# Casting k's main rows into DRAM in blocks of 16 KB instead of 4 KB

## The chip, the cores and the metric

The kernel runs on one core of a Trainium2 chip. The core has a matrix engine (TensorE, PE in the profile, with its weight loads as PEld), VectorE (DVE), ScalarE (ACT), GpSimd (POOL) and SyncE (SP), and 16 DMA engines that carry out the transfers which SP, ACT and POOL issue. Each engine works through its own list of instructions in order and waits for others by semaphores. The metric is the device time in microseconds (us).

## The reference

Eight batches of random-feature attention over 576 positions and 8 heads of 64, followed by a token-and-channel mixer:

```python
def phi(x):                                   # x: b h 576 64, scaled by 64 ** -0.25
    h = einsum('bhsd,md->bhsm', x, omega) - sum(x * x, -1, keepdims=True) / 2
    return exp(h - max(h, -1, keepdims=True)) / sqrt(128)
q_p, k_p = phi(q_s), phi(k_s)
kv, z = einsum('bhsm,bhsd->bhmd', k_p, v), sum(k_p, axis=2)
x = einsum('bhsm,bhmd->bhsd', q_p, kv) / (einsum('bhsm,bhm->bhs', q_p, z)[..., None] + 1e-6)
x = x.transpose(0, 2, 1, 3).reshape(8, 576, 512)
h = maximum(x.transpose(0, 2, 1) @ w_tok1, 0) @ w_tok2      # mixes positions, 576 -> 256 -> 576
u = x + h.transpose(0, 2, 1)
out = u + maximum(u @ w_ch1, 0) @ w_ch2                     # mixes channels, 512 -> 1536 -> 512
```

## The kernel before

The matrix work is in fp16 with sums in fp32. A batch b goes through attention, the token mixer and the channel mixer. The stages of neighbouring batches are interleaved: TensorE computes the channel mixer of one batch between the attention steps of the next. The interleaving is written out by hand: every step is a job, and the list `ORDER` gives the order in which all jobs are recorded, so each engine's list of instructions is fixed. TensorE has no choice at run time. If the next matmul's operand is late, it waits, and all its later work waits with it.

Attention needs q and k with the 64 head dimensions on the partitions. Batches 0 and 1 are transposed on TensorE from natural loads. For batches 2 to 7 the function `load_transposed` goes through DRAM. A DMA issued by POOL casts fp32 to fp16 into a scratch tensor `scratch[w, b]` of 2304 rows of 128 fp16 values (two positions of 64 side by side). Then SP issues a transposing DMA (line 400, `back`), which writes `kT` or `qT` with 128 partitions. The casts are these:

- q: one DMA of the whole batch (line 379, `cast`), 32 pieces of 9216 values.
- k's main rows (line 384, `cast_main`), the first 512 positions of each of the 8 heads: 512 KB of fp16 from 1 MB of fp32.
- k's tail rows (line 390, `cast_tail`): the last 64 positions, two DMAs of 32 KB, each from four heads.

`back` for k waits for the main cast and both tail casts; `back` for q waits for the q cast. SP's list is in order too. It holds, beside the kT and qT transposes, the transposes `uT<-u` (line 824), which turn the token mixer's output into the stationary operand of the channel mixer, and part of the output stores. POOL's list holds all casting DMAs (v, the casts above, the v tails `vt`), and between them the products `vs` and other elementwise work that waits for DVE.

On TensorE, line 571 (k's tail rows) and line 679 (k's main rows) read `kT`; lines 641 and 691 read `qT`; line 1144 reads `uT` for the channel mixer of batches 1 to 4 and line 1073 for later ones. `kT`, `qT` and `uT` have three buffers each.

Of the kernel before, what the change touches and what calls it, by code (L numbers as in the profile page):

```python
# [137 lines left out]
class Planner:  # L138
# [38 lines left out]
    def place(self, tag, name):  # L177
        return self.held[tag, name]
# [7 lines left out]
def kernel(  # L186
# [14 lines left out]
    B, H, S, D = q.shape  # L201
# [4 lines left out]
    P = 128  # L206
    SM = 512
    ST = S - SM
    NJ = SM // P
# [4 lines left out]
    R = SM // 2  # L214
# [84 lines left out]
    scratch = {}  # L299
# [3 lines left out]
    src = {"q": q, "k": k}  # L303
# [26 lines left out]
    def dma(eng, key, wire, fn, deps=(), take=(), give=(), cost=None):  # L330
        cost = (0.75 if eng == "POOL" else 0.45) if cost is None else cost
        job = add(eng, cost, key, fn, deps, take, give, wire=wire)
        return job
# [41 lines left out]
    def load_transposed(b, key, deps=()):  # L375
        casts = {"q": [], "k": []}
        for n, w in enumerate("qk"):
            def cast(w=w):
                nc.gpsimd.dma_start(
                    out=scratch[w, b].rearrange("(p r) e -> p (r e)", p=P),  # L380
                    in_=src[w][b].rearrange("h s d -> (h s d)").rearrange("(p f) -> p f", p=P),
                )
            def cast_main(w=w):
                nc.gpsimd.dma_start(
                    out=scratch[w, b][0 : H * R].rearrange("(h c r) e -> c h (r e)", h=H, c=P // H),
                    in_=src[w][b, :, 0:SM, :].rearrange("h s d -> h (s d)").rearrange("h (c f) -> c h f", c=P // H),
                )
            def cast_tail(w=w):
                for g in range(2):
                    nc.gpsimd.dma_start(  # L390
                        out=scratch[w, b][H * R : H * RA, g * D : (g + 1) * D],
                        in_=src[w][b, 4 * g : 4 * g + 4, SM:S, :],
                    )
            if w == "k":
                casts[w].append(dma("POOL", key + 0.01 * n - 0.005, 0.8, cast_tail, deps, cost=1.1))
            casts[w].append(dma("POOL", key + 0.01 * n, 3.2, cast if w == "q" else cast_main, deps, cost=0.55))
        for n, w in enumerate("qk"):
            def back(w=w):
                t = (t_qT if w == "q" else t_kT)[place(w + "T", b)]
                nc.sync.dma_start_transpose(out=t.unsqueeze(1), in_=scratch[w, b])  # L400
            ld[w + "T", b] = dma("SP", key + 0.2 + 0.01 * n, 2.2, back, deps=casts[w], take=[(w + "T", b)], cost=2.5)
# [25 lines left out]
    def clear(t):  # L427
# [6 lines left out]
        out=w1m.rearrange("p j t -> p (j t)"), in_=moe_w_tok1[0:SM, :].rearrange("(p j) t -> p (j t)", j=NJ)))  # L434
# [23 lines left out]
    for i in range(2):  # L458
        c0 = i * (NCB // 2)
        j_wc2.append(dma("POOL", -3.0 + 0.1 * i, 3.85, lambda c0=c0: nc.gpsimd.dma_start(  # L460
            out=wc2[:, c0 : c0 + NCB // 2, :], in_=moe_w_ch2[c0 * P : (c0 + NCB // 2) * P, :].rearrange("(i p) d -> p i d", p=P))))
# [5 lines left out]
    for out_, a, b in ((T1, W12, W11), (T2, W22, T1), (T3, W22, W12), (T4, W21, T2)):  # L467
# [3 lines left out]
        out=omega16.rearrange("p (i d) -> p i d", i=2), in0=omega_nat.unsqueeze(1).broadcast_to((P, 2, D)), scalar1=c_scale, scalar2=None, op0=ALU.mult), deps=j_om)  # L471
# [779 lines left out]
```

## Time and profile before

| | before |
|---|---|
| median of 3 runs | 274.45 us (273.89 to 274.65) |
| the profiled execution's own time | 273.79 us |
| its span, first to last instruction | 272.0 us |
| granted TensorE clock, mean | 0.998 |
| TensorE busy | 262.9 us, 97% of the span |
| VectorE, ScalarE, POOL busy | 84%, 60%, 49% of the span |
| DMA moved | 39.70 MB in 81296 packets |
| the six casts of k's main rows | 512 KB each, median 7.1 us from issue to landing |

The profile shows one execution. Times in it are us from the span's start. A row of the timeline gives start, duration, engine, line of the kernel, operation, and what is written from what. Sequencer rows (SPq, and POOL's DMA rows) show the issuing instruction alone; the time to landing is given apart. The DMA share of a window is the busy share of all 16 DMA engines together, where 1.00 is 16 engines busy with one packet each; packets of two queues can overlap on one engine, which gives shares above 1.

### The profile page before, as it was taken

What the parts mean: (1) busy time and instruction counts of PE and PEld (TensorE: products, weight loads), DVE (VectorE), ACT (ScalarE), POOL (GpSimd) and SP (SyncE); (2) the same over time, 40 slices, a digit from 0 to 9 for tenths busy, and PEclk for the clock granted to TensorE, in tenths of its full rate; (3) what the DMA queues carried; (4) which work ended last, traced back from release to release, by engine and by line L of the source; (5) the groups of instructions that cost most, each with busy time, mean ns of one, the idle gap of its engine ahead of it and who ended that gap; (6) DMA issues with size and microseconds to landing.
All of it is one profiled execution on the core that took longest, in us unless ns stands there. A gap on an engine that the chain in (4) does not pass through costs nothing.

```text
span 272.0 us, 6648 instructions
## 1 busy us (share of the span) xinstructions
PE 262.9 (97%) x2647; PEld 180.0 (66%) x2647; DVE 227.2 (84%) x479; ACT 164.2 (60%) x361; POOL 134.6 (49%) x146
## 2 busy tenths in 40 slices
PE   7799999999999999999999999999999999999992
PEld 4367455444568655766578546986789688888881
DVE  3897879876998799987889799899997795799992
ACT  2999941188695338736746865699947541573500
POOL 8895492064803490079459996964145044600001
PEclk9999999999999999999999999999999999999999
DMA  8999999999999999989989986980260063030134
GB/s 199 190 208 210 191 210 185 216 202 132 180 204 156 223 187 175 164 160 158 171 178 173 194 233 64 182 167 2 49 128 2 23 193 58 0 157 0 63 133 119
DMA packets 81296, 39.70 MB, mean 146 GB/s; under 512 B 63984, under 2 KB 77040, under 8 KB 81072
## 3 DMA queue, kind: packets, MB, share of 16 engines
q0 software_dynamic: 31744, 17.74, 44.2%
q1 hardware_dynamic: 46928, 15.37, 29.5%
q10 hardware_dynamic: 2592, 6.16, 6.4%
q8 instruction: 20, 0.33, 0.5%
q14 instruction: 12, 0.10, 0.1%
HBM read 35.95 MB, written 16.52 MB: 193 GB/s over the span
## 4 chain that ended last, share of the span: by engine, by line
PE 86%; DMA 8%; POOL 3%; DVE 1%; issue 0%; POOLq 0%; SPq 0%
PE bank L961 24%; PE bank L1144 19%; PE bank L1073 13%; PE bank L803 5%; PE bank L816 5%; DMA uT<-u 4%; DMA w1m<-in_moe_w_tok_dram 4%; PE bank L1178 4%; PE bank L679 3%; PE bank L768 3%; PE bank L735 3%; PE bank L691 2%; POOL r L339 1%; PE bank L870 1%; PE bank L842 1%; PE bank L854 1%
## 5 line engine op out<-in xcount | busy, mean ns | idle before, releaser
L1144 PE MATMUL bank<-uT,wc 128*128 128x512 f16 x232 | 56.0, 379 | 0.0
L315 POOL TENSOR_TENSOR vs<-v,vs 128x512 f16<-128x512 f16 x31 | 33.1, 1072 | 42.8 <-DVE vs L716 33.5
L310 ACT ACTIVATE r<-bank 128x512 f16<-128x512 f32 (+1 forms) x61 | 34.5, 598 | 26.5 <-PE bank L1144 16.0
L961 PEld LDWEIGHTS <-r 128*128 128x128 f16 x384 | 36.7, 98 | 7.2 <-issue 1.6
L534 ACT ACTIVATE kp<-bank 128x512 f16<-128x512 f32 x64 | 35.5, 623 | 9.6 <-PE bank L679 8.9
L712 DVE TENSOR_REDUCE km<-kp 128x8 f16<-128x1024 f16 x32 | 38.5, 1204 | 2.0 <-ACT kp L534 2.0
L534 ACT ACTIVATE qp<-bank 128x512 f16<-128x512 f32 x64 | 36.5, 620 | 4.3 <-PE bank L691 4.3
L1144 PEld LDWEIGHTS <-wc 128*128 128x128 f16 x232 | 20.5, 98 | 20.1 <-issue 1.1
L961 PEld LDWEIGHTS <-S 128*128 128x128 f16 x288 | 27.7, 98 | 4.7 <-issue 0.4
L786 DVE TENSOR_TENSOR x<-bank,rc 128x320 f16<-128x320 f32 x53 | 25.2, 483 | 1.1
L941 DVE TENSOR_TENSOR o<-u,bank 128x512 f32<-128x512 f16 x28 | 19.1, 680 | 5.8 <-PE bank L961 5.3
L961 PE MATMUL bank<-T,r 128*128 128x256 f16 x192 | 23.8, 273 | 0.0
L961 PE MATMUL bank<-T,S 128*128 128x256 f16 x192 | 23.4, 272 | 0.0
L961 PE MATMUL bank<-wc,r 128*128 128x256 f16 x192 | 23.1, 273 | 0.0
L312 DVE TENSOR_SCALAR r<-bank 128x512 f16<-128x512 f32 (+1 forms) x29 | 18.9, 661 | 3.1 <-PE bank L1144 2.4
L819 DVE TENSOR_TENSOR u<-x,bank 128x512 f16<-128x512 f16 x28 | 17.9, 681 | 1.9 <-PE bank L816 1.9
L315 POOL TENSOR_TENSOR vbd<-vt,vbd 128x512 f16<-128x512 f16 x6 | 6.4, 1060 | 23.5 <-DVE vbd L616 18.5
L768 PEld LDWEIGHTS <-qp 128*128 128x128 f16 x256 | 14.0, 98 | 5.9 <-issue 0.3
L1073 PE MATMUL bank<-uT,wc 128*128 128x256 f16 x120 | 16.6, 273 | 0.6 <-DMA uT<-u 0.6
L941 DVE TENSOR_TENSOR o<-o,bank 128x512 f32<-128x512 f32 x21 | 14.3, 680 | 3.1 <-PE bank L961 2.9
L775 DVE RECIPROCAL rc<-bank 128x5 f32<-128x5 f32 x64 | 11.2, 184 | 6.7 <-PE bank L770 3.7
L768 PE MATMUL bank<-kvsb,qp 128*128 128x65 f16 x256 | 16.0, 193 | 0.2 <-ACT qp L534 0.2
(151 smaller groups left out, 551.3 us busy)
## 6 DMA issues: line engine op xcount, KB each, us to landing
out_dram<-o ACTq DMA_DIRECT2D x9, 512.0 KB, 3.7
q<-in_q_dram POOLq DMA_DIRECT2D x6, 576.0 KB, 7.6
wc<-in_moe_w_ch_dram POOLq DMA_DIRECT2D x4, 768.0 KB, 11.1
k<-in_k_dram POOLq DMA_DIRECT2D x6, 512.0 KB, 7.1
v<-in_v_dram POOLq DMA_DIRECT2D x6, 512.0 KB, 8.6
out_dram<-o SPq DMA_DIRECT2D x5, 512.0 KB, 3.1
r<-in_q_dram POOLq DMA_DIRECT2D x4, 288.0 KB, 7.1
v<-in_v_dram POOLq DMA_DIRECT2D x4, 256.0 KB, 8.9
```

The costliest lines, as they stand in the source:

```text
L310: nc.scalar.activation(out=out, in_=in_, func=AF.Relu)
L312: nc.vector.tensor_relu(out=out, in_=in_)
L315: (nc.gpsimd if eng == "POOL" else nc.vector).tensor_tensor(**kw)
L534: nc.scalar.activation(out=out, in_=in_, func=AF.Exp, bias=0.0, scale=1.0)
L712: nc.vector.reduce_max(out=t_km[place("km", (b, hp))], in_=src_, axis=AX.X)
L768: nc.tensor.matmul(ps[:, k, j * 65 : (j + 1) * 65], st, s[:, i, 0 : D + 1], start=True, stop=True)
L786: nc.vector.tensor_tensor(out=to, in0=ps, in1=rc.unsqueeze(2).broadcast_to((P, NJ + 1, D)), op=ALU.mult)
L819: nc.vector.tensor_tensor(out=t_u[place("u", b)][:, j, :], in0=t_x[place("x", b)][:, j, :], in1=bank(n), op=ALU.add)
L941: nc.vector.tensor_tensor(out=o, in0=a, in1=ps, op=ALU.add)
L961: nc.tensor.matmul(ps[:, j * DH : (j + 1) * DH], a[:, cb, j * P : (j + 1) * P], w[:, cb, :], start=(bank_of(b, j0) not in held and j == j0 ...
L1073: nc.tensor.matmul(ps[:, n, :], w(a)[:, (2 * m + n) * P : (2 * m + n + 1) * P], x_[:, a], start=(what in ("P1", "P2", "P5") and n == 0 and ...
L1144: nc.tensor.matmul(ps, wc1[:, db, cb * P : (cb + 1) * P], moving(db), start=(db == 0), stop=(db == ND - 1))
```

## The change

`cast_main` walks the same bytes in another shape. A head's 512 positions are 32768 consecutive values in the source, and 256 consecutive rows of 128 in the scratch tensor. Before, they were cut into `c = P // H = 16` blocks of 2048 values (4 KB of fp16, 8 KB of fp32); now into `c = NJ = 4` blocks of 8192 values (16 KB of fp16, 32 KB of fp32). The block index c is the outermost dimension of both access patterns, the head the next, and the block's values the innermost.

```diff
             def cast_main(w=w):
                 nc.gpsimd.dma_start(
-                    out=scratch[w, b][0 : H * R].rearrange("(h c r) e -> c h (r e)", h=H, c=P // H),
-                    in_=src[w][b, :, 0:SM, :].rearrange("h s d -> h (s d)").rearrange("h (c f) -> c h f", c=P // H),
+                    out=scratch[w, b][0 : H * R].rearrange("(h c r) e -> c h (r e)", h=H, c=NJ),
+                    in_=src[w][b, :, 0:SM, :].rearrange("h s d -> h (s d)").rearrange("h (c f) -> c h f", c=NJ),
                 )
```

No instruction is added, removed or moved on any engine; only the pattern of the six DMAs of line 384 is another. At the first of them POOL's list reads as follows, with the line, the operation, the names of what is written and read (the name's last numbers are buffers; `k_2_152` is the scratch tensor of batch 2) and the counts of the written pattern, outermost first:

```order
 L315 TENSOR_TENSOR T<-vt_94,T 128x16x64
 L315 TENSOR_TENSOR vs_105<-v_91,vs_105 128x8x64
-L384 DMA k_2_152<-in_k_dram 16x8x2048
+L384 DMA k_2_152<-in_k_dram 4x8x8192
 L315 TENSOR_TENSOR vs_103<-v_91,vs_103 128x8x64
 L371 DMA vt_93<-in_v_dram 64x4x64
```

Nothing moved here; the outermost count went from 16 to 4, the innermost from 2048 to 8192. The other five casts of k's main rows differ in the same way.

## The prediction

> **What bounds the kernel now.** I read the engines' busy times first, then what TensorE waits for, then the DMA issues, and last the places where a cast of k ends in something that TensorE reads.
>
> ```profile
> PE 262.9 (97%) x2647; PEld 180.0 (66%) x2647; DVE 227.2 (84%) x479; ACT 164.2 (60%) x361; POOL 134.6 (49%) x146
> ```
>
> This row of the page is the busy time of each engine, its share of the span and its instructions. TensorE is busy for 97% of the span. The list of TensorE's waits has seven rows, of which these are the longest and the longest one on a DMA:
>
> ```profile
> PE bank L1218 <- DVE S L1215: 1.2, 1, 1.2
> ...
> PE bank L1073 <- DMA uT<-u: 0.6, 2, 0.3
> ```
>
> The columns are the total in us, the number of waits and the longest. TensorE never waits more than 1.2 us, and never for a DMA into kT or qT. So any delay of an operand beyond its slack is added to the time one for one: there is no idle time on TensorE in which it could be made up. The question is how much later the casts land and how much slack stands behind each.
>
> **What one cast costs.** A window in which a cast of k's main rows has the DMA engines to itself, then the q cast and the k cast of the issue table:
>
> ```profile
> 90.20:92.20 2.00, 2.00 (x22) 1.34 (x21) 1.65 (x3) 0.96 (x4) 0.75 (x2) 1.00 0.99 200
> ```
> ```profile
> q<-in_q_dram POOLq DMA_DIRECT2D x6, 576.0 KB, 7.6
> ...
> k<-in_k_dram POOLq DMA_DIRECT2D x6, 512.0 KB, 7.1
> ```
>
> The window's last two numbers are the DMA share, 0.99 of 16 engines, and 200 GB/s written. 524,288 bytes at 200 GB/s are 2.6 us, with all 16 engines at work. Size of block alone changes little: the q cast, in blocks of 18 KB, moves 12% more bytes and lands in 7% more time (7.6 against 7.1 us). What matters is how many of the 16 engines share the work when the outermost count is 4 and not 16. The trace names no engine of a packet, so I bound it from both sides. Low end: the 32 blocks are dealt to 16 engines, two each; 2.6 us, no change. High end: one engine for each outermost index, four engines at a sixteenth of 200 GB/s each, 50 GB/s, so 10.5 us, that is 7.9 us more. The nearest row to an outermost count of 4 is the tail cast, whose source pattern begins with four heads, against the v tail, whose pattern begins with 64 or more:
>
> ```profile
> L390 POOL DMA_DIRECT2D k<-in_k_dram x12: 816/850/897, 40.0 to 162.2; - x12
> ...
> DMA to landing us min/median/max: 5.1/6.8/8.9
> ```
> ```profile
> L371 POOL DMA_DIRECT2D vt<-in_v_dram x16: 615/676/754, 3.9 to 180.9; - x16
> ...
> DMA to landing us min/median/max: 2.3/5.9/11.1
> ```
>
> Both move 32 KB in pieces of 128 bytes. The v tail can land in 2.3 us, the tail cast never in less than 5.1. One writes to SBUF and one to DRAM, so it is no proof, but it points to fewer engines. I take the high end, 7.9 us.
>
> The Trainium skill, "DMA: Bandwidth & Descriptors", section on why a DMA increments its semaphore by 16, says that a transfer runs on the largest number of engines, up to 16, that divides the outermost count of both patterns. By that rule the new cast has four engines and the sum is the one below. No row of this profile shows the number itself.
>
> **Where the casts end.** POOL's issues of the six casts, and what SP does with them:
>
> ```profile
> 36.12 0.60 POOL L384 DMA_DIRECT2D k<-in_k_dram  x1
> ...
> 60.30 0.56 POOL L384 DMA_DIRECT2D k<-in_k_dram  x1
> ...
> 87.22 0.59 POOL L384 DMA_DIRECT2D k<-in_k_dram  x1
> ...
> 99.59 0.58 POOL L384 DMA_DIRECT2D k<-in_k_dram  x1
> ...
> 122.37 0.56 POOL L384 DMA_DIRECT2D k<-in_k_dram  x1
> ...
> 147.41 0.57 POOL L384 DMA_DIRECT2D k<-in_k_dram  x1
> ```
> ```profile
> 47.81 2.71 SPq L400 DMA_TRANSPOSE kT<-k  x1
> 50.57 2.34 SPq L400 DMA_TRANSPOSE qT<-q  x1
> 54.30 1.73 SPq L824 DMA_TRANSPOSE uT<-u  x1
> ...
> 66.27 3.30 SPq L400 DMA_TRANSPOSE qT<-q  x1
> 69.75 3.20 SPq L400 DMA_TRANSPOSE kT<-k  x1
> ...
> 93.93 3.15 SPq L400 DMA_TRANSPOSE kT<-k  x1
> 110.41 3.12 SPq L824 DMA_TRANSPOSE uT<-u  x1
> 113.71 2.88 SPq L400 DMA_TRANSPOSE kT<-k  x1
> ...
> 135.63 5.13 SPq L400 DMA_TRANSPOSE kT<-k  x1
> ...
> 170.63 3.18 SPq L400 DMA_TRANSPOSE kT<-k  x1
> ```
>
> Landing times (shortest, median, longest) of all casts of line 384, of all kT and qT transposes of line 400, and of all uT transposes of line 824, in this order:
>
> ```profile
> L384 POOL DMA_DIRECT2D k<-in_k_dram x6: 557/574/601, 36.1 to 147.4; - x6
> ...
> DMA to landing us min/median/max: 6.5/7.1/9.2
> ```
> ```profile
> DMA to landing us min/median/max: 4.5/6.7/9.3
> ```
> ```profile
> DMA to landing us min/median/max: 5.1/5.6/6.4
> ```
>
> And the first use on TensorE in batches 2, 3 and 4 (kT, uT; qT, kT; kT):
>
> ```profile
> 54.84 0.29 PE L571 MATMUL bank<-omT,kT 64*128 64x128 f16 x4
> ...
> 60.50 1.69 PE L1144 MATMUL bank<-uT,wc 128*128 128x512 f16 x7
> ```
> ```profile
> 74.03 0.28 PE L641 MATMUL bank<-qT,omT 64*128 64x256 f16 x2
> ...
> 78.05 0.61 PE L679 MATMUL bank<-omT,kT 64*128 64x128 f16 x16
> ```
> ```profile
> 107.38 0.39 PE L679 MATMUL bank<-omT,kT 64*128 64x128 f16 x8
> ```
>
> The casts' own times of issue hardly move (POOL spends about 0.57 us on each either way). Each lands 7.9 us later. What else POOL issues behind a cast (q cast, v, tails) stands behind it on the four engines.
>
> **Batch 2.** Issue at 36.12 and the median of 7.1 give a landing at 43.2; with 7.9 more, 51.1. SP starts kT at 47.81 in the profile, so 3.3 us later. kT landing at 51.1 plus 4.5 (the shortest transpose) to 6.7 is at 55.6 to 57.8, against 54.84: a stall of 0.8 to 3.0 us. SP's list goes on behind it: qT starts at 51.1 + 2.71 = 53.8 at the earliest, uT at 53.8 + 2.34 = 56.2, and uT lands 5.6 us later, at 61.8, against 60.50; 1.3 us, of which the first stall is a part. The q cast and the v load are queued behind k's cast on the four engines and hold them when these transposes come, so I take the upper end, 3.0.
>
> **Batch 3.** The longest landing, 9.2 us, belongs to this cast: 60.30 + 9.2 = 69.5, just ahead of kT at 69.75. Now 77.4. kT then lands at 81.9 to 84.1 for a first use at 78.05: 3.9 to 6.1 us. Before that, qT (issued at 66.27) runs into the cast: four of the 16 engines are busy till 77, and a transpose is complete when its last engine is. If its part on the four engines waits for the cast, it lands no earlier than about 77 + 2 (less than the shortest transpose's 4.5, since the other engines' part is done), for a use at 74.03: 5 us, in which kT's delay is contained at its middle value. I take 5.0 for both.
>
> **Batch 4.** kT starts at 93.93, 6.7 us after the cast's issue at 87.22 and so, with a median landing of 7.1, as soon as the cast has landed; now 101.8. kT lands 4.5 to 9.3 us later, at 106.3 to 111.1, against 107.38: 0 to 3.7 us. I take 2.0.
>
> **Batches 5 to 7.** Batch 5's cast, issued at 99.59, lands at 106.7 (median) to 108.8 (longest), now 114.6 to 116.7; kT starts at 113.71 at present, up to 3 us earlier. The first uses in batches 5 and 6:
>
> ```profile
> 128.49 0.62 PE L679 MATMUL bank<-omT,kT 64*128 64x128 f16 x16
> ```
> ```profile
> 144.59 0.28 PE L571 MATMUL bank<-omT,kT 64*128 64x128 f16 x4
> ```
>
> 128.49 hides batch 5. But uT, issued at 110.41 and landing at 115.5 to 116.8, runs into the longer cast, as qT does in batch 3: 0 to 2 us, taken as 1.0. Batch 6: 122.37 + 7.1 + 7.9 = 137.4 against a start at 135.63, 1.8 us late, for a use at 144.59; with 6.7 us to land, 144.1, it just fits: 0. Batch 7: 147.41 + 7.1 + 7.9 = 162.4 against a start at 170.63: hidden. The v loads behind that cast are late, and POOL already waits for one:
>
> ```profile
> POOL vs L315 <- DMA v<-in_v_dram: 2.7, 1, 2.7
> ```
>
> POOL's products feed TensorE, so I put 0 to 3 there and take 1.0. **Sum:** 3.0 + 5.0 + 2.0 + 1.0 + 0 + 1.0 = 12.0 us.
>
> **The clock.** After TensorE's last matmul the granted clock is:
>
> ```profile
> 267.50:270.00 2.50, 0.00 (x0) 0.00 (x0) 0.00 (x0) 0.00 (x0) 0.00 (x0) 1.00 0.85 240
> 270.00:272.00 2.00, 0.00 (x0) 0.00 (x0) 0.00 (x0) 0.00 (x0) 0.00 (x0) 0.78 0.01 5
> ```
>
> The column ahead of the DMA share is the clock: 1.00 for 2.5 us without a matmul, then 0.78 on average over the next 2 us. A stall of 4 or 5 us in batch 3 can therefore reach a lowered clock, which makes the matmuls after it slower for some time. I bound it by 0 and 3 us in all, and take 1.0. The Trainium skill, "TensorE: Matmul & The Clock Gate", Part 1, states half the clock after an idle window of about 3.4 us and full clock after as much busy time; this profile's drop, 2.5 us or more after the last matmul, agrees, and the way back is shown by no row here.
>
> So 13 us. The sum is made on the profiled execution, 273.79 us with a span of 272.0, which is 0.66 us below the median of the runs, 274.45; against that median the forecast is 287.5 us.
>
> **The rivals.** *Sixteen engines all the same* (the change does not reach the engines' share): two blocks of 16 KB on each, 2.6 us, nothing is late, 274.4 us. For it speaks the q cast, whose few large pieces land as fast as k's many small ones. Against it speaks the tail cast's 5.1 us. At best the larger blocks are 5% cheaper a byte (the q cast's 12% more bytes in 7% more time), 0.13 us of 2.6, six times, 0.8 us if none were hidden: not slower, and the one case that could be faster. It decides if a cast's landing stays near 7 us. *Four engines, mostly hidden*: transposes flow beside the cast on the other engines and catch up, and only kT of batches 2 and 3 is late at the low bounds, 0.8 + 3.9 = 4.7 us, giving 279; for it speaks the low bound 0 in batches 4 to 7. *Caught behind the next cast*: kT of batch 4, started at 101.8 and not at 93.93, meets the cast of batch 5 (issued at 99.59), and if that cast gets its engines first, kT lands after 116.5 + 2, which is 11.1 us behind 107.38 and 9.1 more than the 2.0 taken; with the rest of the clock's 3 us, 298. For it speaks that transposes take 4.5 to 9.3 us: they lose time to other transfers already. A like collision can arise in batches 6 and 7.
>
> **How the numbers follow.** Four engines and the sum above, 282 to 293: 0.54. Caught behind the next cast, over 293: 0.23. Mostly hidden, 275.3 to 282: 0.14. Sixteen engines: 0.09, of which 0.02 are faster by over 0.3%. A measurement of this kernel tells about 0.3%, 0.8 us, from no change. So slower 0.91, same 0.07, faster 0.02. The range is 279 to 300: it leaves out the sixteen engines (0.09), the lower part of the hidden case (0.06) and 0.04 at the top; the likeliest case's own range is 282 to 293.
>
> **What would show it.** In the changed profile the landing of line 384's DMA should read 14 to 17 us instead of 6.5 to 9.2, and a window inside a lone cast should show a DMA share near 0.25 and some 50 GB/s. TensorE's waits should name DMA kT and qT, with some 3 us at 55 and 4 to 6 us between 74 and 83, and smaller ones after 100; its busy time should stay near 263. The clock row should show a dip after the stall of batch 3 or none. A landing still near 7 us proves the step on the engines wrong; a landing of 15 us with TensorE's waits below 3 us proves the slack wrong.

## The result, and the profile after

The changed kernel takes 334.63 us (median of 6 runs, 332.54 to 348.75) against 274.25 us (273.81 to 280.57) for the kernel before beside it: 1.219 times, with a 95% interval of 1.211 to 1.228. The forecast was 287.5 us with a range of 279 to 300. Executions of one kernel scatter: the profiled one here, 348.75 us with a span of 347.0 us, is the longest of the six, so its waits are read for their place and cause and not for the time, and every ratio in this document leaves out executions more than 1.5% above the shortest of their kernel.

Busy time by engine, and the row of the granted TensorE clock (40 slices of 8.7 us, tenths of full speed), of the changed kernel:

```profile
PE 274.3 (79%) x2647; PEld 184.7 (53%) x2647; DVE 228.3 (66%) x479; ACT 164.4 (47%) x361; POOL 135.0 (39%) x146
...
PEclk9999998799579996557999969957999999999998
```

TensorE was busy for 97% of the span and is now busy for 79%. What it waits for (total, number, longest):

```profile
PE bank L679 <- DMA kT<-k: 26.2, 1, 26.2
PE bank L691 <- DMA qT<-q: 14.2, 1, 14.2
PE bank L571 <- DMA kT<-k: 13.1, 2, 7.0
PE bank L641 <- DMA qT<-q: 11.0, 1, 11.0
```

Before, no wait was longer than 1.2 us. Now five waits for transposing DMAs take 64.5 us. TensorE's idle time rose from 272.0 - 262.9 = 9.1 us to 347.0 - 274.3 = 72.7 us, that is by 63.6, and its busy time by 11.4 for the same 2647 instructions: 75.0 us, the whole difference of the two profiled spans (the medians of the runs differ by 60.4). The 11.4 us go with the clock: wherever the clock row shows a 5 or 6, a wait has just ended or is still on, and right behind the second wait eight matmuls of line 803 take 3.60 us, before 1.90. A window inside the longest of these waits has the clock (third number from the end) at half:

```profile
140.00:150.00 10.00, 0.00 (x0) 0.00 (x0) 0.00 (x0) 0.00 (x0) 0.00 (x0) 0.50 1.77 22
```

That is the half speed which the Trainium skill, "TensorE: Matmul & The Clock Gate", Part 1, gives for an idle TensorE. The same row holds the riddle of this case: in these 10 us the DMA engines are occupied (share 1.77, more than all 16) and move only 22 GB/s.

The casts themselves do what was forecast. Line 384, with the time to landing, was 6.5 / 7.1 / 9.2 and is now:

```profile
L384 POOL DMA_DIRECT2D k<-in_k_dram x6: 602/646/664, 36.0 to 200.2; - x6
...
DMA to landing us min/median/max: 13.5/14.7/32.3
```

The median is 7.6 us longer, where 7.9 was forecast. That four engines carry a cast can be counted here too: a landing is sixteen increments of a semaphore, and for batch 2's cast twelve of them came by 41.5 us and four between 49.9 and 51.2. The longest, 32.3, is not explained by a cast alone. The five waits in order of time, from the timeline (the wait stands in brackets):

```profile
61.83 0.39 PE L571 MATMUL bank<-omT,kT 64*128 64x128 f16 x4 [7.01 <-DMA kT<-k]
...
93.65 0.39 PE L641 MATMUL bank<-qT,omT 64*128 64x256 f16 x2 [11.04 <-DMA qT<-q]
...
156.07 0.61 PE L679 MATMUL bank<-omT,kT 64*128 64x128 f16 x8 [26.25 <-DMA kT<-k]
...
201.65 0.40 PE L571 MATMUL bank<-omT,kT 64*128 64x128 f16 x4 [6.05 <-DMA kT<-k]
...
234.40 0.61 PE L691 MATMUL bank<-qT,omT 64*128 64x512 f16 x2 [14.19 <-DMA qT<-q]
```

They belong to batches 2, 3, 4, 6 and 6. The DMAs behind the second, third and fifth, each by its own issue, with the time to landing as the last number:

```profile
qT<-q SPq DMA_TRANSPOSE x1, 20.0
...
v<-in_v_dram POOLq DMA_DIRECT2D x1, 512.0 KB, 32.9
k<-in_k_dram POOLq DMA_DIRECT2D x1, 512.0 KB, 32.3
...
kT<-k SPq DMA_TRANSPOSE x1, 33.1
...
qT<-q SPq DMA_TRANSPOSE x1, 33.2
```

A transpose that took 4.5 to 9.3 us before takes 20.0, 33.1 and 33.2 us. Each was issued while a cast of k was in flight or about to start: qT of batch 3 at 73.62, inside batch 3's cast (67.40 to 84.08); kT of batch 4 at 122.97, with batch 5's cast issued at 121.89; qT of batch 6 at 201.19, with batch 7's cast issued at 200.25.

### The profile page after: what moved, and what is told of

It reads as the page before. It is cut to its first block, busy times and chain, and to the rows that moved or that the text cites. A ratio compares the mean times of both kernels' runs of the same rounds, so it can differ in the third digit from the quotient of the medians.

```text
span 347.0 us, 6648 instructions
## 1 busy us (share of the span) xinstructions
PE 274.3 (79%) x2647; PEld 184.7 (53%) x2647; DVE 228.3 (66%) x479; ACT 164.4 (47%) x361; POOL 135.0 (39%) x146
## 4 chain that ended last, share of the span: by engine, by line
PE 50%; DMA 40%; ACT 3%; POOL 2%; DVE 2%; issue 1%; POOLq 0%; DVEq 0%; SPq 0%
PE bank L961 17%; DMA qT<-q 15%; DMA kT<-k 15%; PE bank L1073 11%; DMA k<-in_k_dram 8%; PE bank L1144 4%; PE bank L803 4%; PE bank L816 3%; PE bank L679 2%; DMA uT<-u 2%; PE bank L691 1%; POOL vs L315 1%; ACT kp L534 1%; PE bank L768 1%; PE bank L1178 1%; PE bank L735 1%
## 5 line engine op out<-in xcount | busy, mean ns | idle before, releaser
L315 POOL TENSOR_TENSOR vs<-v,vs 128x512 f16<-128x512 f16 x31 | 33.1, 1071 | 104.9 <-DVE vs L716 81.0
L961 PEld LDWEIGHTS <-r 128*128 128x128 f16 x384 | 37.7, 100 | 8.6 <-issue 2.9
L679 PE MATMUL bank<-omT,kT 64*128 64x128 f16 x256 | 12.1, 228 | 26.7 <-DMA kT<-k 26.2
L961 PEld LDWEIGHTS <-S 128*128 128x128 f16 x288 | 28.4, 100 | 5.6 <-issue 1.0
L1144 PEld LDWEIGHTS <-wc 128*128 128x128 f16 x232 | 20.6, 98 | 20.1 <-issue 1.1
L679 PEld LDWEIGHTS <-kT 64*128 64x128 f16 x256 | 8.4, 99 | 31.5 <-DMA kT<-k 26.5
L961 PE MATMUL bank<-T,r 128*128 128x256 f16 x192 | 25.1, 282 | 0.0
L961 PE MATMUL bank<-T,S 128*128 128x256 f16 x192 | 24.6, 281 | 0.0
L691 PE MATMUL bank<-qT,omT 64*128 64x512 f16 x64 | 12.2, 395 | 14.2 <-DMA qT<-q 14.2
L534 ACT ACTIVATE qpt<-bank 128x512 f16<-128x512 f32 (+1 forms) x16 | 11.2, 716 | 15.6 <-PE bank L641 15.6
## 6 DMA issues: line engine op xcount, KB each, us to landing
k<-in_k_dram POOLq DMA_DIRECT2D x6, 512.0 KB, 14.7
```

The source lines that it names most:

```text
L315: (nc.gpsimd if eng == "POOL" else nc.vector).tensor_tensor(**kw)
L534: nc.scalar.activation(out=out, in_=in_, func=AF.Exp, bias=0.0, scale=1.0)
L679: nc.tensor.matmul(ps[e][:, c : c + M], m[half[e], r, :], omT[half[e]], start=True, stop=True)
L961: nc.tensor.matmul(ps[:, j * DH : (j + 1) * DH], a[:, cb, j * P : (j + 1) * P], w[:, cb, :], start=(bank_of(b, j0) not in held and j == j0 ...
L1144: nc.tensor.matmul(ps, wc1[:, db, cb * P : (cb + 1) * P], moving(db), start=(db == 0), stop=(db == ND - 1))
```

## The experiments

Two theories stood at the start, and the expectations call them by letters. M: a transposing DMA that meets a cast confined to four engines is slowed as a whole, far beyond its own part on those four. L: it only has to wait for the cast's end and lands a microsecond or two after it, and the delays of the kernel come from the order of issues. Later came H, that a transpose is held on all 16 engines while such a cast is in flight, against Q, that it is held on the cast's four engines alone. All ratios are against the kernel before, run on the same chip beside it. The kernels of transfers alone (e1, e5, e9, e13) were run once each; where two of them hold the same group of transfers, they agree within 0.4 us.

### One cast and one transpose, by themselves (e1_micro)

```diff
+    phases = [
+        ("lone", None, True),
+        ("sixteena", lambda d, b: blocks(d, b, 16), False),
+        ("foura", lambda d, b: blocks(d, b, 4), False),
+        ("foursmalla", four_small, False),
+        ("sixteen", lambda d, b: blocks(d, b, 16), True),
+        ("four", lambda d, b: blocks(d, b, 4), True),
+        ("foursmall", four_small, True),
...
+    for n, (name, cast, with_t) in enumerate(phases):
...
+            cast(d, 1 + n % 7)
...
+            nc.sync.dma_start_transpose(out=t.unsqueeze(1), in_=base)
```

`blocks(d, b, c)` is the cast of line 384 with outermost count c; `four_small` has outermost count 4 and 32 pieces of 2048 values (4 KB) in each. A barrier stands behind each phase, and the transpose reads a scratch tensor that was complete long before, so the two DMAs have nothing to wait for but the engines.

> A kernel of its own that leaves out the whole computation and writes zeros: nine phases, each fenced off from the next, with a cast of k's main rows (512 KB) alone, a transposing DMA of 2304 rows alone, or both started together. Theory M (meeting): a transposing DMA that meets a cast on four engines is slowed far beyond the cast's end, because each of its packets on those engines stands behind a 16 KB piece and the others keep step. Then the lone transpose lands in about 5 us, the lone cast in 7 (16 blocks outermost) and 14 to 15 us (4 outermost), and the transpose beside the 4-outermost cast of 16 KB pieces in 20 to 33 us; beside a 4-outermost cast of 4 KB pieces in 10 to 20; beside 16 outermost in 6 to 9. Rival L (late landing alone): the transpose ends about 2 us after the cast does, 15 to 17 us beside both 4-outermost casts. Rival S (size of the pieces, not the number of engines): the lone cast of 4 KB pieces with 4 outermost lands in about 7 us and slows the transpose no more than 16 outermost does; the 18 KB pieces of the whole-batch cast slow it most.

Time to landing of each DMA (a name that ends in "a" is a cast alone):

```profile
castsixteena<-in_k_dram POOLq DMA_DIRECT2D x1, 512.0 KB, 5.2
castfoura<-in_k_dram POOLq DMA_DIRECT2D x1, 512.0 KB, 12.0
castfoursmalla<-in_k_dram POOLq DMA_DIRECT2D x1, 512.0 KB, 12.5
...
turnlone<-base SPq DMA_TRANSPOSE x1, 4.4
...
turnsixteen<-base SPq DMA_TRANSPOSE x1, 7.3
...
turnfour<-base SPq DMA_TRANSPOSE x1, 14.8
...
turnfoursmall<-base SPq DMA_TRANSPOSE x1, 14.9
```

The outermost count sets the number of engines, and that sets the time: 5.2 us with 16, 12.0 with 4. The size of the block does next to nothing: four engines with pieces of 4 KB need 12.5. Beside the transpose, a cast on 16 engines in pieces of 4 KB makes it 7.3 us, the q cast in pieces of 18 KB 7.5, and a cast on eight engines 9.5, so rival S falls. The Trainium skill, "DMA: Bandwidth & Descriptors", section on why a DMA increments its semaphore by 16, gives four engines for this pattern, and the trace agrees: 50 GB/s at a DMA share of 0.25 in the middle of the cast with 4 KB pieces, as forecast; the 16 KB pieces read 55 and 0.26 in e9 below. A transpose issued 0.2 us ahead of the four-engine cast lands 1.1 us after it (14.75 us against 13.44 from its issue 0.22 us later). So for the pair alone L is right: 15 us, and not the 20 to 33 of M.

### Casts with outermost count 4 in pieces that use all engines, and 8 engines (e2, e6, e3, e7, e8)

e2: the same 16 KB blocks, but each cast cut into four DMAs of two heads; e6 is the same cut with the old 4 KB blocks, to price the cut itself.

```diff
-                nc.gpsimd.dma_start(
-                    out=scratch[w, b][0 : H * R].rearrange("(h c r) e -> c h (r e)", h=H, c=P // H),
...
+                for h in range(0, H, 2):
+                    nc.gpsimd.dma_start(
+                        out=scratch[w, b][h * R : (h + 2) * R].rearrange("(h c r) e -> c h (r e)", h=2, c=NJ),
+                        in_=src[w][b, h : h + 2, 0:SM, :].rearrange("h s d -> h (s d)").rearrange("h (c f) -> c h f", c=NJ),
+                    )
```

(e6: `c=P // H` in both.)

> The same 16 KB blocks, but as four DMAs of two heads each with 4 blocks outermost: 8 pieces a DMA on four engines, two pieces an engine, and the four DMAs on different engines if these are taken in turn. Three more issues of about 0.6 us on POOL for each batch. Theory M and rival L (engines matter): each cast lands in 8 to 11 us, and the time is 275 to 282 us. Rival S (16 KB pieces matter): transposes that meet it still take over 15 us and the time stays above 295 us.

> The control of the four DMAs of two heads: 4 KB blocks with 16 outermost, as in the kernel before, and also four issues in place of one. If the loss of 2% with 16 KB blocks in four DMAs is POOL's three more issues, this has the same time, 278 to 282 us. If 16 KB pieces cost something by themselves: 274 to 276 us.

e2 takes 280.44 us, 1.020 [1.014, 1.025]; e6, with the old blocks, 278.02 us, 1.010 [1.006, 1.014]. Line 385's DMAs in e2:

```profile
DMA to landing us min/median/max: 5.5/7.0/9.4
```

With 16 KB blocks in four DMAs of 128 KB, each lands 7.0 us after its own issue, about as the whole cast did before the change. Half of the 2% is the price of the cut: POOL issues 24 DMAs for 6, and POOL's products vs come late (three waits, 4.3 us in all, in e2's profiled execution of 285.27 us). Some 1% is left between e2 and e6, which no run takes apart; it is not the 22% of the change. That four four-engine DMAs issued one after another land so soon also suggests that they don't share the same four; e9 shows it below.

e3 takes outermost count 8 with 8 KB blocks (`c=2 * NJ`), e7 outermost count 8 with larger blocks (the head outermost, `"h c (r e)"` and `"h c f"` with `c=NJ`; the trace has them as pieces of 32 KB), and e8 count 32 with 2 KB blocks (`c=8 * NJ`).

> 8 blocks of 8 KB outermost: eight engines if the outermost count sets them. A lone cast then needs 5.2 us of engine time and lands in about 10 us, 2.6 more than before. Theory M: transposes that meet it take 8 to 15 us, and the time is 280 to 300 us. Rival L: only the landings are 2.6 us later, 275 to 279 us. If the number of engines were not set by the outermost count: a landing of 7 us and 274 us.

> The head outermost and four blocks that lie one behind the other, which the DMA takes as two pieces of 32 KB: eight engines, two pieces an engine, twice the largest piece so far. If the time on the engines decides and not the size of the pieces, it is as the eight engines with 8 KB, 283 to 295 us, with a landing near 10 us. If the size of the pieces decides: over 320 us.

> Blocks of 2 KB, 32 outermost: all 16 engines. If the number of engines decides: 274 to 276 us. If smaller pieces let transposes pass sooner and that were worth something here: below 273 us.

e3: median 289.86 us (283.2 to 300.88 in four runs). e7: median 288.76 us (285.83 to 296.97), 1.041 [1.037, 1.045]. e8: 274.82 us, 1.002 [0.999, 1.004]. In the profiled executions of e3 and e7 (290.53 and 296.97 us) TensorE's longest waits are again for kT, 6.7 and 11.7 us.

Four times the piece at the same eight engines makes no difference that can be told from the scatter (the shortest runs are 283.2 and 285.8 us, the medians 289.9 and 288.8), and half the block at 16 engines makes none at all. Sixteen, eight and four engines give 274.3, 283 to 290 and 334.6 us: the cost grows faster than the engine time in a cast, 2.6 us on 16 engines and, estimated from it, 5.2 and 10.5 on eight and four.

### Keeping the transposes off the casts (e4_guard)

```diff
+    def guard():
+        while unseen:
+            s = unseen.pop(0)
...
+            nc.sync.dma_start(out=t_guard[:, n : n + 1], in_=s[0:16, 0:1])
...
+                unseen.append(scratch[w, b])
...
+                guard()
```

The changed kernel, with a call of `guard` ahead of each transpose on SP (lines 400 and 824): for each cast of k recorded so far and not yet guarded, a DMA of 32 bytes that reads the cast's scratch tensor and therefore waits for it.

> The changed kernel with one more small DMA on SP ahead of a transpose of kT, qT or uT: it reads 16 values of the scratch tensor of each cast recorded since, so SP waits until that cast has landed and the transpose cannot meet it. That covers qT of batch 3 with the cast of batch 3, and qT of batch 6 and uT with the cast of batch 7; kT of batch 4 still meets the cast of batch 5, which is recorded later. Theory M: the guarded transposes fall from 20 and 33 us to 5 to 8 us, SP waits longer ahead of them, and the time falls by 10 to 25 us against the changed kernel, to 310 to 325 us. Rival L: waiting longer can only cost, 334 us or more.

339.24 us (333.4 to 342.9), 1.220 [1.210, 1.229]: nothing gained, which L had said and M had not. A new wait has taken the place of the old:

```profile
PE bank L1156 <- DMA uT<-u: 23.3, 1, 23.3
```

(Line 1156 is line 1144 of before.) The uT transpose, held back on SP by the guard of a later cast, is late instead. The guarded qT transposes fall from 20.0 and 33.2 us to 11.8 and 11.0, not to the 5 to 8 that M expected, and that uT takes 14.3; q and v transfers are queued behind each cast and come at the same time, and e9 below has a crowd without any four-engine cast that costs as much. The guard moved the wait, and by itself it doesn't separate the theories.

### Crowds around the pair (e5_micro_crowd)

```diff
+    phases = [
+        ("va", "v", False, False), ("vfoura", "v4", False, False), ("vfour", "v4", True, False), ("vsixteen", "v6", True, False),
+        ("fourv", "4v", True, False), ("storea", "", False, True), ("fourstorea", "4", False, True),
+        ("fourstore", "4", True, True), ("sixteenstore", "6", True, True), ("fourfour", "45", True, False),
+    ]
```

The second field is what POOL issues, in order: v is a load of v, 4 and 5 are casts with outermost count 4, 6 one with 16. The two that follow say whether SP issues a transpose and ScalarE a store.

> Again a kernel that leaves out the whole computation: ten phases that add to the cast and the transpose a v load of 512 KB from POOL (v) or a store of 512 KB from ACT that starts some 5 us later. Theory H (held): while a transpose is in flight beside a cast on four engines, all 16 engines are held to one packet of the transpose for each 16 KB piece, so that other transfers wait too, on all engines. Then the v load ahead of the cast lands in 6 to 8 us alone and beside the cast without a transpose, and in 12 us or more when a transpose is added; the store lands in 3 to 6 us alone, in 8 to 12 beside the cast alone, and not before the cast's end beside both; and two casts on four engines each beside one transpose take 22 us or more together. Rival Q (queue): each transfer waits only for its own part on the four engines: v ahead of the cast is not slowed by the transpose, the store is slowed as much without the transpose as with it, and two casts on different engines take about 14 us together.

A four-engine cast, the load of v issued behind it, and the transpose beside both; and an output store alone and beside a four-engine cast:

```profile
castfourv<-in_k_dram POOLq DMA_DIRECT2D x1, 512.0 KB, 13.9
loadfourv<-in_v_dram POOLq DMA_DIRECT2D x1, 512.0 KB, 19.8
out_dram<-holdstorea ACTq DMA_DIRECT2D x1, 512.0 KB, 2.7
...
out_dram<-holdfourstorea ACTq DMA_DIRECT2D x1, 512.0 KB, 9.5
...
turnfourv<-base SPq DMA_TRANSPOSE x1, 20.4
```

With a v load behind the cast the transpose needs 20.4 us in place of 14.8. With the v load ahead of the cast it needs 7.2, and so does that load, where H had expected 12 or more: a transpose that is well ahead of the cast's pieces is not held. So what stands behind the cast matters: here are the 20 us that the kernel shows for batch 3. Even a store on another queue needs 9.5 us in place of 2.7, without any transpose.

### Is the transpose held on all engines, or on four? (e9_micro_pairs)

```diff
+    phases = [
...
+        ("foursa", "45", False, False),
...
+        ("fours", "45", True, False),
...
+    ]
```

Two casts on four engines each, without and with a transpose that is issued 0.2 us ahead of them; other phases have a v load in the place of the second cast, or both.

> The whole computation is left out here as well. Eight phases: a four-engine cast with a v load behind it, two four-engine casts one behind the other, and cast, v load and cast, each without and with a transpose beside them; and the last two with a transpose and casts on 16 engines. Theory H (a transpose in flight holds all 16 engines to the pace of the busy four): two casts without a transpose run on different engines at the same time, both landed after 14 to 16 us, with a transpose after 22 or more; the v load behind one cast lands in 14 to 16 us without a transpose and in 19 to 21 with it; cast, v load and cast: the second cast lands in 15 to 18 us without and 25 to 35 with it. Rival Q (only the four engines are busy): the transpose adds no more than 3 us to any of these. On 16 engines all land within 8 to 14 us.

Time to landing, first without, then with the transpose:

```profile
castfoursa<-in_k_dram POOLq DMA_DIRECT2D x1, 512.0 KB, 12.6
againfoursa<-in_k_dram POOLq DMA_DIRECT2D x1, 512.0 KB, 13.6
...
castfours<-in_k_dram POOLq DMA_DIRECT2D x1, 512.0 KB, 12.8
againfours<-in_k_dram POOLq DMA_DIRECT2D x1, 512.0 KB, 22.6
...
turnfours<-base SPq DMA_TRANSPOSE x1, 17.4
...
turnsixteenvsixteen<-base SPq DMA_TRANSPOSE x1, 15.7
```

Windows of the same kernel (DVE and POOL busy, clock, DMA share, GB/s): the two casts without the transpose, then with it, and the second cast when the transpose's packets have run:

```profile
30.00:36.00 6.00, 0.00 (x0) 0.00 (x0) 1.00 0.52 109
68.00:74.00 6.00, 0.00 (x0) 0.00 (x0) 1.00 1.31 58
78.00:84.00 6.00, 0.16 (x1) 0.00 (x0) 1.00 0.26 55
```

Without the transpose the two casts run side by side on eight engines, 109 GB/s, and land within 1.7 us of each other. The second therefore has four engines of its own. (The Trainium skill, "DMA: Bandwidth & Descriptors", section on why a DMA increments its semaphore by 16, says that a DMA issued by POOL on fewer than 16 engines takes the next ones in turn.) With a transpose in flight the second cast does not start until the first has ended, though by the phase without a transpose it has other engines: 22.6 us. The transpose is the only difference between the two phases. The other phases agree: a v load behind a four-engine cast lands in 15.3 us without and 20.1 with the transpose, and the second cast of cast, v load and cast in 16.0 and 28.3. In the window from 68 to 74, 82 packets of the transpose ran on all engines together:

```profile
q1 hardware_dynamic: 82, 0.02, 104.6%
q0 software_dynamic: 20, 0.33, 26.3%
```

That is 14 packets of 256 bytes per us, where 935 ran in the microsecond from 64.5 to 65.5, at whose end the first 16 KB pieces began. Counted in the trace, a 16 KB piece takes 1.23 us and a transpose packet in that time 1.24 us (medians from 67 to 75 us): about 16 packets each time that the four engines finish a piece each. The trace names no engine of a packet, so that this is one packet on each engine is read from the counts; that the second cast is held on engines of its own is what decides. H holds and Q falls. The Trainium skill, "DMA: Bandwidth & Descriptors", section on queues, rings and completion order, lets each engine change between its queues packet by packet; by that alone twelve engines would have been free, and the trace shows that they are not. The Trainium skill, "Advanced Engine Details and Errata", section X-Bar Transpose, speaks of a transpose's wavefronts of 16 rows; 16 packets for each round of pieces fit that, but no run here looks inside.

The last line of the landing times is a control that missed its expectation of 8 to 14 us: cast, v load and cast, all on 16 engines, and the transpose beside them still takes 15.7 us. So a crowd behind the transpose costs it about as much as one lone four-engine cast does (14.8 in e1), and with both it takes 20.1.

### When the transpose starts (e13_micro_late)

```diff
+    phases = [
+        ("lateno", 0, 4096, 0), ("latefour", 4, 4096, 0), ("laterfour", 4, 8192, 0),
+        ("latesixteen", 16, 2048, 0), ("aheadfour", 4, 0, 1536), ("fartherfour", 4, 0, 3072),
+    ]
```

The fields are the outermost count of the cast, the width of a ScalarE copy that holds the transpose back, and the width of a POOL memset that holds the cast back.

> The whole computation is left out; the output is zeros. One transpose of 576 KB at a time, started at another time beside a cast of 512 KB: 4 us and 8 us into a cast with outermost count 4, 2 us into one with outermost count 16, and 1 and 3 us (rough) ahead of a cast with outermost count 4. The prediction's step (the twelve other engines' part is done by the cast's end): the transpose started inside the cast lands about 2 us after the cast. Theory H (the transpose is held on all engines while the cast's pieces are in flight): it lands 4 to 10 us after the cast's end, whenever it was started inside it, since almost none of it is done by then. A transpose started 1 us or more ahead of the cast has most of its packets done when the cast's pieces begin: by H 5 to 9 us in all, well ahead of the cast's end at 3 us ahead. A third reading (engines are shared packet by packet, only the four busy ones are slow): landing about at the cast's end in every case, also where the transpose is ahead.

```profile
castlatefour<-in_k_dram POOLq DMA_DIRECT2D x1, 512.0 KB, 12.8
...
turnlatefour<-base SPq DMA_TRANSPOSE x1, 11.3
...
turnlaterfour<-base SPq DMA_TRANSPOSE x1, 7.5
...
turnaheadfour<-base SPq DMA_TRANSPOSE x1, 7.4
...
turnfartherfour<-base SPq DMA_TRANSPOSE x1, 4.1
```

Started 3.6 us and 7.3 us into the cast (22.89 and 42.18 against 19.25 and 34.89), the transposes land 34.22 and 49.68, both 2.2 us after the cast (32.03 and 47.45). Started 1.3 us ahead, the transpose lands 7.3 us before the cast. So the 2 us of the prediction are right for a lone pair, and H's expectation of 4 to 10 us was wrong there. The third reading falls with the transposes that started ahead. But the 2 us come about otherwise than the prediction had it. Packets of the transpose (q1) while the cast ran, from 24 to 31, and in the 2.3 us behind it:

```profile
q1 hardware_dynamic: 443, 0.11, 101.9%
```
```profile
q1 hardware_dynamic: 1720, 0.42, 82.5%
```

During these 7 us of the cast only 443 packets ran, 403 of them in the first 2 us of the seven; 1720 had to run when the cast was done, and could, because nothing else asked for the engines.

### One batch at a time (e14, e15, e10, e11, e12, e16)

Outermost count 4 in the named batches alone, 16 in the others:

```diff
-                    out=scratch[w, b][0 : H * R].rearrange("(h c r) e -> c h (r e)", h=H, c=P // H),
+                    out=scratch[w, b][0 : H * R].rearrange("(h c r) e -> c h (r e)", h=H, c=NJ if b in (2,) else P // H),
```

The pattern read has the same. This is e14; e15 has `(3,)`, e10 `(4,)`, e11 `(5,)`, e12 `(4, 5)` and e16 `(6, 7)`.

> Outermost count 4 in batch 2 alone. The prediction's term for batch 2 is 3.0 us: 277.5. Theory now: SP's transpose of kT waits for the two tail casts as well, which stand behind the main cast and land 3.8 us after it, so it starts at 55.1 and the wait at line 571 is 7 us: 281 to 283 with something for the clock.

> Outermost count 4 in batch 3 alone. The prediction's term is 5.0 us: 279.5. Theory H: the qT transpose starts in the middle of the cast, is held on all engines until the cast ends at about 77 and takes 5 to 9 us more, and the v load behind has to follow: a wait at line 641 of 9 to 12 us, 284 to 288.

> Only the cast of batch 4 in 16 KB blocks. It lands some 7 us later, kT of batch 4 too; its first use has 4.4 us of slack. All theories: TensorE waits 2 to 5 us for kT, 277 to 280 us.

> Only the cast of batch 5 in 16 KB blocks. kT of batch 4 is started as before and is through before this cast reaches the DMA engines; the cast's own landing is not needed until 113. All theories: 274 to 277 us.

> The casts of batches 4 and 5 in 16 KB blocks. kT of batch 4 then starts late enough to meet the cast of batch 5. Theory H: that transpose takes 17 to 33 us, and the time is 290 to 305 us, far above the sum of the two alone. If the losses only add: 277 to 283 us.

> Outermost count 4 in batches 6 and 7. The prediction's terms are 0 and 1.0: 275.5. Theory H: kT of batch 6 starts behind the tails at 138 to 139 and lands at 144 to 147 for a use at 144.6, 0 to 2.5 us; qT of batch 6, started near the cast of batch 7, has to be read at 161.4 and is late only if it starts after that cast: then 4 to 10 us. 275 to 287; the two waits of the changed kernel in these batches (6.0 and 14.2 us) come back here in full only if they don't hang on the delays of the batches before.

The longest waits of these, in the timeline of e14, e15, e10, e12 and e16 (two):

```profile
61.42 0.40 PE L571 MATMUL bank<-omT,kT 64*128 64x128 f16 x4 [6.76 <-DMA kT<-k]
```
```profile
86.53 0.39 PE L641 MATMUL bank<-qT,omT 64*128 64x256 f16 x2 [11.98 <-DMA qT<-q]
```
```profile
118.10 0.61 PE L679 MATMUL bank<-omT,kT 64*128 64x128 f16 x8 [9.77 <-DMA kT<-k]
```
```profile
122.82 0.61 PE L679 MATMUL bank<-omT,kT 64*128 64x128 f16 x8 [13.89 <-DMA kT<-k]
```
```profile
150.12 0.39 PE L571 MATMUL bank<-omT,kT 64*128 64x128 f16 x4 [3.77 <-DMA kT<-k]
...
185.42 0.61 PE L691 MATMUL bank<-qT,omT 64*128 64x512 f16 x2 [16.79 <-DMA qT<-q]
```

| count 4 in batch | time, us (runs) | ratio, 95% interval | more than before, us: by the median of all runs; by that of the runs within 1.5% of the shortest |
|---|---|---|---|
| 2 | 282.48 (281.6 to 283.5) | 1.028 [1.025, 1.031] | 8.1; 8.1 |
| 3 | 292.03 (289.2 to 295.1) | 1.054 [1.051, 1.057] | 17.7; 15.1 |
| 4 | 287.24 (287.0 to 287.5) | 1.046 [1.042, 1.050] | 12.7; 12.7 |
| 5 | 280.60 (278.3 and 282.9) | none | 6.0; 3.7 (one run) |
| 4 and 5 | 291.27 (291.2 to 291.4) | 1.061 [1.057, 1.064] | 16.7; 16.7 |
| 6 and 7 | 294.57 (283.7 to 300.8) | none | 20.2; 9.3 (one run) |
| all | 334.63 (332.5 to 348.8) | 1.219 [1.211, 1.228] | 60.4; 58.9 |

Batches 2, 3, 4 with 5, and 6 with 7 add up to 62.7 us by the medians of all runs, and to 49.2 by the last column's second number, against 60.4 and 58.9 for the change of all of them. So the parts account for most of the cost. Whether some 10 us more come from an effect across the batches is not settled by these runs: batches 6 and 7 scatter by 17 us, and e16's waits of 3.8 and 16.8 us are those of an execution of 300.75 us; they can't both stand in the one of 283.7.

Batch 4 alone was expected at 277 to 280 and takes 287.2: its kT, issued at 102.0 and not at 93.9, starts behind a crowd (the q cast, v, three vt, batch 5's cast and, just behind it, its tails) that it used to precede, and lands 16.0 us later although batch 5's cast has its 16 engines. With batch 5's cast on four, 20.3 us. So, by these two runs (12.7 us of 16.7), most of the cost of these two batches is the late start into a crowd, as in e9's control, and the smaller part is the four-engine cast that it meets. The expectation for both together was 290 to 305 (H) or 277 to 283 (the losses only add): 291.3 is in the first range, but the two alone, 12.7 and 3.7 to 6.0, add up to 16.4 to 18.7 and both together cost 16.7, so H's "far above the sum of the two alone" did not come.

Batch 5 alone was expected at 274 to 277 and takes 278.3 and 282.9. The wait in its profile (of the longer run) is for no transpose:

```profile
PE bank L961 <- DVE o L941: 3.0, 1, 3.0
...
out_dram<-o ACTq DMA_DIRECT2D x1, 512.0 KB, 9.2
```

VectorE waited 3.4 us for the buffer o, which an output store issued at 110.12, inside the cast, still read. Such a store had a median of 3.7 us before and here takes 9.2, like the store beside the four-engine cast in e5. uT, issued inside the same cast at 112.73, lands in 9.9 us (before, in 6.4 at most), and TensorE doesn't wait for it.

## Why the prediction was wrong

- **The step on the engines: right.** Four engines, 12.0 us against 5.2 for a cast alone, a landing of 14.7 us (forecast 14 to 17). The price per cast was right to 0.3 us, and the rival "sixteen engines all the same" falls. Its evidence, the tail cast's row, was read a little too simply: four of the 16 v tails, those of batches 0 and 1, begin with four heads in the source too. The 2.3 us belongs to one of the other twelve, so the comparison stands.
- **The step that failed: the landing of a transpose that meets a cast, in batch 3.** The prediction had it land "no earlier than about 77 + 2 (less than the shortest transpose's 4.5, since the other engines' part is done)". The other engines' part is not done: during the cast a transpose moves some 14 packets per us over all engines (e9), so nearly all of it is still to come. In e15 itself 64 packets of qT ran from 68 to 75 us, of some 2300. In a lone pair it catches up in 2.2 us (e13). In the kernel it meets, at the cast's end, the q cast, the tails, vt and v loads that POOL had issued behind the cast; in e5 a v load there makes the same difference, 20.4 us against the 14.8 of e1. In e15, where only batch 3 is changed, the cast lands at 77.74, almost exactly at the forecast's 77.4, and qT at 86.48, 8.7 us after it: a wait of 12.0 us for the 5.0 forecast. In the changed kernel it is 9.5 us after (84.08 and 93.60).
- **Batch 2, 3.0 forecast, 7.0 measured.** The cast landed at 51.21 (forecast 51.1). But kT's transpose waits for the tail casts too, which POOL issues behind the main cast and q's cast. Of the sixteen increments of the second tail, twelve had come by 46.6 us and four came from 53.6 to 55.01, right behind the last four of q (52.8 to 54.2) and of the main cast: the four busy engines. SP issued kT at 55.10; 6.7 us to land makes 61.8, the row at 61.83. The prediction named what is queued behind the cast and left the tails out of the sum. Its own profile had shown them: before the change kT started at 47.81 although the main cast had landed at 43.7, since SP was waiting for a cast of k until the tails had landed at 47.7:

```profile
SPq L400 <- DMA k<-in_k_dram: 47.0, 2, 45.6
```

qT and uT, which it feared, cost nothing there.
- **Batches 4 and 5, 2.0 and 1.0 forecast, 26.2 measured.** The rival "caught behind the next cast" named the place and mechanism (kT of batch 4 beside batch 5's cast); it had a chance of 0.23 and was priced at 9.1 us more. The place was right and the size too small: 13.9 us with these two batches changed, 26.2 with all. The mechanism was right in part: 9.8 us come with batch 5's cast on 16 engines (e10), from the late start among ordinary transfers. The doubling from 13.9 to 26.2 is seen in one execution only, the longest, 14 us over the median, and no trace of a shorter one was kept. In it, counted in the trace, the 32 pieces of batch 5's cast form four chains of eight. Two chains end at 138 us and one at 142. The fourth ends at 151.5, because its first piece took 12.1 us (130.75 to 142.89) where others take 1.23, and its other seven ran behind it one by one; from 143 to 151 the transpose moved some 14 packets per us. In e12 all four chains end by 116.5, after 10.5 us. Why one piece took 12 us is open. Batch 5's own term, a late uT, was not what cost time in e11: an output store was.
- **Batches 6 and 7, 0 and 1.0 forecast, 6.0 and 14.2 measured** (3.8 and 16.8 in e16). "A like collision can arise in batches 6 and 7", the prediction said, and put nothing in the sum for it. kT of batch 6 waits for the tails as in batch 2 and takes 10.4 us (in e16: main cast landed at 138.3, kT issued at 139.70). qT of batch 6 used to start 3.4 us ahead of batch 7's cast (144.03 and 147.41); behind the late kT and uT it starts 0.9 us after it (149.91 and 149.00 in e16), and takes 35.5 us. These are the sizes of single executions, and e16 scatters by 17 us.
- **The clock, 1.0 forecast with a bound of 3, 11.4 us measured** as more busy time. The bound was made for one stall of 4 to 5 us; there were five, of 6 to 26 us, in that execution. A single stall costs it about 3 us: 3.1 in e14 (266.0 us busy, 262.9 before) and 2.6 in e15 (265.5). "Busy near 263" was wrong for the same reason.
- **No slack on TensorE: right.** In e14 TensorE is idle for 6.6 us more than before (its one new wait is 6.8) and busy for 3.1 more, and the span is 9.7 us longer (281.7 against 272.0): nothing was made up.
- **The range** took each collision as a single late landing with a fixed price, and most of them as absent. Five waits of 6 to 26 us, each with its clock, do not fit in it.

Block size, which the change is named for, is not the cause: 16 KB blocks on all engines cost 2% (e2), of which half is the cut, and e1, e7 and e8 agree. What stays open, beside that piece of 12 us and the 10 us that the single batches leave, is why a transpose on the hardware queue is held on engines that have no piece of the cast; the runs show that it is.

## What to carry to other kernels

Look at the outermost count of both patterns of a DMA before its block size: it sets the number of engines, and e1 shows 12.0 us (pieces of 16 KB) and 12.5 (4 KB) for four against 5.2 for 16. A long transfer on few engines costs more than its own length when a transposing DMA can meet it, because that DMA then holds all engines at its pace, and everything queued behind both comes due at once. A transpose that only starts late, into a crowd that it used to precede, pays much of this as well (e10: 16.0 us with the crowd's casts on 16 engines). Where TensorE has no slack, list which transposes will start inside or just behind each later cast, count the tails among the things they wait for, and price every stall with its clock.

## What the runs showed of the hardware

- A transposing DMA beside a cast on four engines runs at 14 packets of 256 bytes per us on all 16 engines together, and at 935 in the microsecond before that cast's pieces begin (e9); in the stall of the changed kernel the engines were occupied at a share of 1.77 and moved 22 GB/s.
- A head start of 1.3 us is enough for the transpose: 7.4 us instead of 11 to 15 (e13, e1). With 2.6 us it is undisturbed (4.1 us).
- Casts on four engines take different engines in turn: two of them issued 0.6 us apart ran side by side, 109 GB/s, until a transpose came between (e9).
- A store of 512 KB from another queue takes 9.5 us beside a four-engine cast and 2.7 alone (e5).
